# Another order-of-issue table for an attention and gated-MLP kernel on one Trainium2 core

## The chip, the core and the metric

The kernel runs on one core of a Trainium2 chip. The metric is the device time of one execution in microseconds (us), lower being better; the time stated is the median of several executions. The profile is one further execution, recorded by the hardware profiler: start and end of every instruction of the five engines (TensorE or PE, VectorE or DVE, ScalarE or ACT, GpSimd or POOL, SyncE or SP) and of the DMA packets.

## The reference

A residual block on x of 2048 tokens by 512 features, in float32. A layernorm feeds two branches, full softmax attention with 32 heads of 16 features, and a gated MLP of width 1792; the output is x + attention * silu(MLP).

```python
def reference(A_x, A_wqkv, A_wo, B_x, B_w1, B_w3, B_w2):
    xn = _layernorm(A_x)                       # 1 x 2048 x 512
    q, k, v = heads(xn @ A_wqkv)               # 32 heads of 16
    p = softmax(einsum("bhqd,bhkd->bhqk", q, k) * 16 ** -0.5)
    s = merge(einsum("bhqk,bhkd->bhqd", p, v)) @ A_wo
    h = silu(xn @ B_w1) * (xn @ B_w3)          # 2048 x 1792
    g = silu(h @ B_w2)
    return A_x + s * g
```

(The names heads and merge stand here for the reshapes and transposes of the original.)

## The kernel before

Operands of the matmuls are split into a high and a low part in a rounded format (float32r), and a product of two such pairs is three matmuls. Only the exponentials times the values are multiplied in plain float32.

There are three stages. The first normalizes and transposes x, makes queries, keys and values and spills them to DRAM. The main stage, which begins 160 us after the first instruction in the profile, works on attention and the MLP at once. The last multiplies by the output weights (`o` in the table), joins the branches and stores.

In the main stage attention goes through 32 phases, a phase being a pair of heads p and a half of the queries (1024). There are four kinds of work for TensorE, and each has a letter:

- `m` / `M` (`max_unit`, line 389): scores of 128 queries by 512 keys into one PSUM bank; VectorE reduces them to a row maximum (line 391). The maxima belong to the phase that comes next.
- `s` / `S` (`scores`, line 627): scores of 128 keys by 512 queries, with the maximum already subtracted by two extra rows of the operands; ScalarE takes the exponential from the bank (line 630) into one of 23 buffers `pt`.
- `v` (`values`, line 640): a value block. Four matmuls multiply four such buffers (two heads, two groups of queries) by 17 columns of values (16 and a column of ones), each in its own 32-column stripe of the array, into the bank `pv`. In plain float32 each is two records in the profile, so a block has eight. 16 blocks make a phase, 512 all of them.
- `f` / `F` (`Lanes.emit`, line 858): the MLP's matmuls, in units of 128 features.

The first, second and fourth kind use half of the array's rows each. A small letter is the lower half (rows 0 to 63, lane 0), a capital the upper half (rows 64 to 127, lane 1). A matmul of each half can run side by side; such a pair is called a slot below. An f product's contraction of 128 is cut into a lower and an upper half; the upper follows the lower into the same bank, and only then is the product done. Value blocks, transposes and the output's products use the whole array, so the halves stop for them. A stretch of whole-array matmuls between two stretches of halves is called a turn.

Seven PSUM banks go around (`take` gives the one that comes free first by the planner's account), and one, `pv`, holds the value sums. So an s or m waits until ScalarE or VectorE has read the bank's last content. A GpSimd pair of instructions splits each unit of MLP weights (lines 321 and 322).

The order in which the kernel issues all this is written out by hand: `ORDER_OF_ISSUE`, a string of letters. The loop at the end of the kernel's function goes through it. An entry that can't go yet (no exponential buffer, no bank, its inputs not due) is put on the list `late` and tried again before each later entry. `r` stands for a value block just ahead of which the finished row maxima of a phase are transposed (`second`, line 404), and `R` for that transposition alone. A small planner (`Model`) keeps due times of banks, lanes and engines while the program is built; they decide what is ready, and when small steps and DMAs are put into the other engines' queues. At run time nothing of it is left but the order of the instructions on each engine, and semaphores.

Of the kernel before, what the change touches and what calls it, by code (L numbers as in the profile page):

```python
# [50 lines left out]
    "MffSfMfSfMfSfSfMfSfMfMfSfMfsMsFFfFffFsMMfMfsFFfFfMsfFfFMsfFmFmFvmMmMFsFffFfFfMFsfFFfFffMSfMffFFmFmfS"  # L51
    "vFmfSFmFfmFfFSfFmFmfFfSfFFmFsFfFfMfMffMMsvSfMfsFfFmFsFMffMsFfFfMsFfFsFMfFsfFMfFfMmvSmmSmFFmvSmmSFmvS"
    "ffMMffSfSFffMSfFfmFsFmFmFFsfFfMfMFmvvSfmMMfFffFsFsFFfFfFsMfsFfFMsfFMfmFSffFMmvSfMfSffMFfSfMffSmFFfsF"
    "mFFsmFFfsFmFmFmFvvvrSfMfSffMfSfSfMsFfFmFsFFmFsFmFsFsFfMfsFfMfSfSFmvmSSmmSvSsmSfMmvfMmSsFmFfFFfSfMfsF"
    "mFFfsFmFfFsFsFMmvvmSMffSMfSffSfMfSfMffMsFFfsFmFFfsFFmFsMffFsFFfMfFmfSmSvSmsSMmvsMMmsFsFvSmsMsMvmSsFs"
    "FMfFffFMsFfmFSfMfFfsMfFFfSfMfSfmFvmSMmmFmFvvvsMfSfFSffMfFFsfMFsfFsMFfFsmFSffFmSFffSrvsMfMfSFffFsFmFf"
    "SFmsFfFfMsFFmFsFmFfSmvmSfSMsMfvmSMmMsvvfMfSSfMfSffMfSfFfMfFsFmFsFsFmFfFsFmFsFfMfFfSmMfSfsMffSsvmSSff"
    "MsMvsSmSmMvvSfMffSfMfSfSfMfMfFfFmFsFfFfFsMfFfSmSfFfFmFsFmFmFsFfFsFfFmSfFmFsFfFfMfMfMsMvsMfMMsvsMSmFm"
    "vSmmFFmmFmFmFvvvmSmFfFFmsFFfmFsFFfsFfMSfFfMfSfMfMfSfFffMsFFfSfMfSfFfMfsFsRvvSmMffSfSfMffSfSmFfFsFmFs"
    "FFfMfFsFfsMFffSMffSfFmSfFsFMfFfSfmFsFsFmFFfmFsFSffFmMvSmsSmMvsFmSmSmFvvmFSmsMsFvsMFmMssFvsMMmsSvsFmS"  # L60
    "FmmSvSmfFmSfSfFFfmSfFmFsFFffSmFsFfFMsfFSfMffFFsmMvsMMmmFmFvvvsMfSfFMfFffSmSfFmFsFfFMfSfMfFfsMfFFssFr"
    "vvSmfFSfFmfSFfmSfFsFMfsFFfmFSffFMsfFFsMffSFfMffMMfsFFfFfMsfFFmFsFfMfmFsFFfMfmFFfMsvvSmsSSmvmSsMvvMff"
    "SSffFMfFssFmFfFsFMfsFFfMfSfmFsFFffFfMSffMSffSfMfFsFfMsFfFmFsFsFmFfFsFmFmFfSmvmSmSSfvmSmMMsvSmSmvSmSf"
    "FfMffFSfmSFfMfsFfFmFsFFfMfsFmFFmFfMfmMvvvMsMsfFfFFsfFMsfFsFFfmFFssFFfMfSffSsFrvvSfMffSfMSffSfMfMfFfS"
    "fFsFmFfFsFmFsFmFsFfFsMfSfFmMvSmmSmFFsvSmmSMsvMsMfsFsFfFFfMsfFFsmFSffFMsFffMfFMfSfMsvmSMmfSvvMfSsfFmF"
    "FfFsmFFfsFMfSffSmFFffSMfFfSfMmvSmFmmFsFvSmmSMsvSmmFfSSffFfFmSfFsFMfFsfFMsfFFsMffSFfMmvSmFmMmvvSfMffM"
    "fSfSfSfMfFfFsFmFsFfFmSfFsMfFfFmFsFmFmMvvrsMFfsFMfFsFfMsFfsFMfSfFfmSfFmFsFmFfFMfMfmSvvSfMfMffSfSfMfSf"
    "FfMfFsMfFsFfMfFsFfMsFsFfFmFsFfMmFfMfSvSmsMMsvSmmSfMvsMMmSffSvvMffSfMfSfMfSfSfFfFmFsFmFsFfSfMfFsFmSFf"
    "FmSfFsFmFfFsMfMfFsMfFsFFsFfFfMfSfMssFvSmMmFsvSmFsmFmSvSmmMsSvSmFsFsmMvSmmFmFsFFmmFmFvvvMsfSMffSfFfFs"
    "MfFFsMffSFffMsFfSMffMFfSfFfSfsMFfFffSSfsSRvvvsMfMMfSffFFffMsFfFFsfMsFfFMfsFmFSfmFFfSffSfFmFmFsFFmFfs"  # L70
    "FmFFfSffMFfsMvvSmSsMmvSmMmfSvvMfmSFmFsfFfFsFmFFfsFsFmFsFFfmFsFFfMsFfsFMfFsFfmMfFSfSfFmvvSmmSfSFfFfFf"
    "mFfSfMfSFffMsFmFfFsFmFMfmFFfMsvvsMfSsFFmFffFMsFfSfmFFsFfsMFfmFfSFfFsmMvSmmSSfvMssSmMvMsSfMfSmvmSMmSs"
    "vvmSfSSfMfFffFSfMffSSfmFFfsFmFFfFsmFsFfMsFmFsRvvSmFfMfSffMFfMfSffFmFmFsFFfFsMfFffFsFFmMmvsMFmsSvMssS"
    "mMvvmFFssFsMFfFfMffSfFMsfFSfMfsFfFmSFffFfSmSvMmsFfFfFfSFmfSfFSmfFfSmFSffFmSfFmFSfmFfFmMvSmMssFvmSsMM"
    "svmSmFsFfSfFFmsFFfmFSfmFfSFmfFMsFfmMvvsMMssMvMsMsfSMfvvMfSffMMfMffSfMfSffFfFsFmFfFsFsFFmFsFffMsFFfMm"
    "RvSmSfSffMfFfFmSfFfSmFsFfFMsfFmFsFMffFsFSfMmvsMMmmFvvSfmFfSSfmFfFSfmFsFFfmSFfFsmFFsFfMmFffMSfvsMfSMs"
    "vvMfSsFfFmFsfFsFmFfFsFsFMffFmFSffFMfmMvvSfMffSfMSffSfMfSfFfFmFsFmFsFfFsFmFfFsMsFfMmFvsMfSfMmSvSmfSsF"
    "FmfFfFsMFffSmFSfFfMsfFmFsFmFfFMfMfMmvvfSMmMmvvsMFmFsFfFsFfmFsFfFsFMfSfMfSffFfMsFsFMfRvMsfMSffSfSfMSf"
    "vMsMfSfSsvmSSfmMvMsSfSfMsvmSfSFfFmFfFsmFFsmFFfsFFmsFFmFfSffMfMSfFffSMfSffFSfmFsFFfmSfFsFMfMffFmMvsMf"
    "MmMvvmMsMFsFsvsMSmSmvsMFsfFSmFffFmFSfmFfSFffMsFFmfFsMFfSffFFmSfFsMfMfFfsFMffFsFfFMfsSvMfSssMMfvsMmMS"  # L80
    "svSmFmmSvSmmFmMmFvvvmSfFsFmFFsfFSmFfsFFmFsfFSmfFmFmFsFFfsFFmFffMSfMfSffMSfRvsMfMfSMfSffMfSfMfSvSmfMs"
    "FsFFfFfMsFfsFmFFsfFmSfFMfmFsFFfsMvSmmSFfFfsFFfmFSfsFmFmFvvvvmSfFFfsSMffFFfFsmFFsfSfMFfFsFmFmfFmSvSmM"
    "mfMSfvSmSfMsvMsMfsFFfFsFfMsFfsFmFfSfFmSfFfSFmfFmFsSvmSSfMfsMvsMmMMmvvvfSMffSfMSffSFfmFsFFfmSfFsFfFMf"
    "SfsFsFmFFfsFrvMsfMfSfFfSFffMfSFmFsMfFfSfmFfFsFmFFfsFmFmMvsMFfsFFmFsFfsFMfSfSfmFFffSmFSffFmFFmMfvSmMs"
    "SfMfvsMMsSsvmFSmSmvvMffSfMfFsMFffSfMFfsFSfmFSfFfmFfFsFFmFffSMfsFfFFmfFSfmFsFfSmFFfmFSfFmfFSfmFmMvvsM"
    "sMsMvsMMfMsvSfMsFmFsFfFfmFFsFmfFSmFfSfMfFfsFMfMfMfFfMmvvvsMSffSfFfFmFsFfFsFmFFsFffSMfFfSfSmFfSfsFrvv"
    "SmfSfFFfSmfFSmFfSffFSmfFSffMsFFfMfsFmFFmFffMsFfFmFFsfFfSmFfSfFFmsFmFfMFsFfmMvmSfSSmvMsMsMsvsMfMMfSsv"
    "sMMsMsvvMffMSfMffSfFsFfFmFsFmFmFSffFmFsFFfmFMffSvsMSsSmvMfMsfFFssFFfmFFsFfsFmFSffSmFfFfSMffMfFSmvmSM"
    "fsMvSmsSFmmFvSmmSMmvvmSSfSfmFfFFfMsfFFsMfsFfFMsfFMffSsFfFMffMfSSffSfMrMsMsvSmmMsSvvSfMffSSffMfMfMfSf"
    "MfsFfFfFFsFmFsFmsFFfMfsFfMfFMsfFFmSfFffMsFmFFfSfmFfFSfmFfFmSvvSmsSmFFmvSmSmMmvvmFsFMfmFsFFfFsFmFfSff"  # L90
    "MFssFfFMfSffMfSfFfSmFfFsFMsFfFsMfFffMFffSfMSmvvsMmMsMvvSfMfSffMfMfSfMfFsFfFsMfFsFfFsMfFmFsFsFfFmFfSf"
    "MmFfSfSfFmFfSfFmFsFmFfSmFfMmvvMsSssFvrvSmfSSfmFfFfFmSFfFsmFFsFfmFsFsFsFmFfFFfmSFfmFsFFfmFSsfFmMvvSmS"
    "sMmvsMMsSfvmSMsSsvmFSfMfFfsMFfFsmFFfSfmFFfSffMfFsFmFfFMmfMvvMffMfSfSfSfFMffFsFFfMsFfFsmFfFFsmSfFFmmF"
    "vsMMmSfvsMsFFfMfFsFfmSFfSfmFFsfFmSFfmFSfSffFMfmFMmvvSsMsmMvvsMfMfSFffSfMSffMfSfMfFsFsFfMFfsFmFsFmFmF"
    "FmFmFsvvsMfFFmsFfFFmMfsFfFfSFfMsFfSfMfFfSfMfFsMRvvsMMffSSffFFfMsFfSfMfsFfFmFsFFmsFFfmFFmfSmSvSmmSSmv"
    "SmMfsSvMssMSmvsMsFFmFfFfSmSfFfMfSfFmSfFfFmSfmFFsmFfFMmvvMsfSMfsMvMsmSsSvMsFmsFsFfFfFmFSffSmFFsFfMfsF"
# [1257 lines left out]
```

## Time and profile before

| | |
|---|---|
| time before, median of 3 runs | 1739.95 us (1739.35 to 1740.43) |
| span of the profiled execution, first to last instruction | 1737.7 us |
| TensorE busy | 1730.3 us, 100% of the span |
| VectorE busy | 1432.1 us, 82% |
| ScalarE busy | 1254.2 us, 72% |
| GpSimd busy | 765.5 us, 44% |

The profiled execution's own time is not listed apart from its span; the median of the timed runs lies 2.25 us above that span. A line of the profile names the source line, the engine, the operation, the tiles as out<-in, the shapes and the count; PEld is the loading of weights into TensorE, which runs beside its matmuls. Ends of matmuls are modelled, so that a matmul of 512 columns is shown with some 0.39 us while the next one of the same half starts 0.23 us after it. Starts are to be trusted.

### The profile page before, as it was taken

The numbers are of one execution on the slowest core, as the hardware profiler recorded it, in microseconds if no ns is written. First come the engines' busy times: TensorE is split into PE (matmuls) and PEld (weight loads), VectorE is DVE, ScalarE is ACT, GpSimd is POOL, SyncE is SP. The second block draws the span as 40 slices with busy tenths as digits, with TensorE's granted clock in tenths as the row PEclk, the third lists the DMA queues.
The fourth block names the chain that finished last, engine by engine and source line by source line (L and its number), as shares of the span: only waits on it lengthen the run. The fifth ranks groups of instructions, "written<-read, shape, count | busy, mean of one in ns | idle before, by whom it ended". The sixth has DMA issues, their size and how long they took to land.

```text
span 1737.7 us, 35616 instructions
## 1 busy us (share of the span) xinstructions
PE 1730.3 (100%) x13236; PEld 1044.5 (60%) x13236; DVE 1432.1 (82%) x2349; ACT 1254.2 (72%) x2440; POOL 765.5 (44%) x793
## 2 busy tenths in 40 slices
PE   9999999999999999999999999999999999999999
PEld 7877656565665555555655655565655555566456
DVE  7567989888888889789888888888988988888535
ACT  4223787878878787778778877887788777777762
POOL 3103653365535560566265623644455515661201
PEclk9999999999999999999999999999999999999999
DMA  8657213122323121222423221132523222421542
GB/s 288 241 205 206 65 33 68 50 69 63 80 84 91 53 72 28 69 66 75 105 74 68 57 63 52 46 72 56 135 56 68 70 35 55 115 76 37 180 152 97
DMA packets 147373, 155.36 MB, mean 89 GB/s; under 512 B 42368, under 2 KB 101760, under 8 KB 144224
## 3 DMA queue, kind: packets, MB, share of 16 engines
q1 hardware_dynamic: 146336, 152.04, 31.7%
q8 instruction: 104, 1.70, 0.4%
q10 hardware_dynamic: 864, 1.05, 0.2%
q14 instruction: 69, 0.57, 0.1%
HBM read 107.97 MB, written 44.02 MB: 87 GB/s over the span
## 4 chain that ended last, share of the span: by engine, by line
PE 98%; DMA 1%; DVE 1%; SPq 0%; ACT 0%; issue 0%; POOL 0%; POOLq 0%; ACTq 0%
PE f L858 28%; PE pv L640 27%; PE e L627 17%; PE m L389 14%; PE m L507 3%; PE e L195 2%; PE e L199 2%; PE e L197 2%; PE o L195 1%; PE o L199 1%; PE o L197 1%; PE m L480 0%; PE m L404 0%; DMA wl<-g 0%; DMA ovl<-o 0%; PE o L1089 0%
## 5 line engine op out<-in xcount | busy, mean ns | idle before, releaser
L391 DVE TENSOR_REDUCE mp<-m 128x1 f32<-128x512 f32 x2048 | 1298.5, 684 | 164.2 <-PE m L389 89.8
L630 ACT ACTIVATE pt<-e 128x512 f32<-128x512 f32 x2048 | 1085.7, 606 | 268.4 <-PE e L627 121.2
L627 PE MATMUL e<-qs,ks 64*128 64x512 f32 x2048 | 716.0, 411 | 0.0
L389 PE MATMUL m<-ks,qs 62*128 62x512 f32 x2048 | 697.8, 413 | 0.0
L640 PE MATMUL pv<-pt,vt 128*17 128x512 f32 x4096 | 508.7, 596 | 0.0
L627 PEld LDWEIGHTS e<-qs,ks 64*128 64x128 f32 x2048 | 344.6, 185 | 228.7 <-ACT pt L630 85.0
L389 PEld LDWEIGHTS m<-ks,qs 62*128 62x128 f32 x2048 | 334.7, 184 | 141.0 <-ACT pt L630 42.8
L640 PEld LDWEIGHTS pv<-pt,vt 128*17 128x17 f32 x4096 | 84.0, 96 | 206.7 <-issue 199.9
L858 PE MATMUL f<-xth,wh 64*128 64x512 f32 x488 | 171.1, 392 | 0.0
L858 PE MATMUL f<-xth,wl 64*128 64x512 f32 x488 | 170.8, 396 | 0.0
L858 PE MATMUL f<-xtl,wh 64*128 64x512 f32 x488 | 169.7, 392 | 0.0
L743 POOL TENSOR_TENSOR h<-g,h 128x512 f32<-128x512 f32 x56 | 72.0, 1286 | 198.8 <-ACT h L739 198.8
L858 PE MATMUL f<-wh,hs 64*128 64x512 f32 x496 | 157.3, 394 | 0.0
L858 PE MATMUL f<-xth,xel 64*128 64x512 f32 x408 | 146.7, 394 | 0.0
L858 PE MATMUL f<-xth,xeh 64*128 64x512 f32 x408 | 143.1, 393 | 0.0
L858 PE MATMUL f<-xtl,xeh 64*128 64x512 f32 x408 | 142.5, 392 | 0.0
L858 PE MATMUL f<-xeh,hs 64*128 64x512 f32 x400 | 122.7, 393 | 0.0
L322 POOL TENSOR_TENSOR wl<-wr,wh 128x512 fp32r<-128x512 f32 x92 | 118.5, 1288 | 7.7
L322 POOL TENSOR_TENSOR xel<-wr,xeh 128x512 fp32r<-128x512 f32 x76 | 98.0, 1289 | 6.3
L727 POOL TENSOR_SCALAR th<-th 128x512 f32<-128x512 f32 x56 | 34.7, 620 | 143.2 <-ACT th L720 143.0
L321 POOL TENSOR_SCALAR wh<-wr 128x512 fp32r<-128x512 f32 x92 | 57.2, 621 | 86.5 <-PE f L858 85.5
L321 POOL TENSOR_SCALAR xeh<-wr 128x512 fp32r<-128x512 f32 x76 | 47.3, 622 | 101.0 <-PE f L858 48.2
(179 smaller groups left out, 2089.5 us busy)
## 6 DMA issues: line engine op xcount, KB each, us to landing
wr<-in_B_w_dram SPq DMA_DIRECT2D x168, 256.0 KB
qs<-qk SPq DMA_DIRECT2D x186, 64.0 KB
ks<-qk SPq DMA_DIRECT2D x90, 128.0 KB
qk<-sh SPq DMA_DIRECT2D x32, 256.0 KB
qk<-sl SPq DMA_DIRECT2D x32, 256.0 KB
v<-vrow SPq DMA_DIRECT2D x16, 272.0 KB
xin<-in_A_x_dram SPq DMA_DIRECT2D x16, 256.0 KB
g<-part SPq DMA_DIRECT2D x16, 256.0 KB
```

Of the source, the lines that this page charges most:

```text
L195: nc.tensor.matmul(ps, lhs[1], rhs[0], start=first, stop=False)
L197: nc.tensor.matmul(ps, lhs[0], rhs[1], start=False, stop=False)
L199: nc.tensor.matmul(ps, lhs[0], rhs[0], start=False, stop=last)
L321: nc.gpsimd.tensor_scalar(hi, t, 1.0, 1.0, op0=ALU.mult, op1=ALU.mult)
L322: nc.gpsimd.tensor_sub(lo, t, raw(hi))
L389: nc.tensor.matmul(ps, qs[p % 2][64 * h:64 * h + KM, q0:q0 + P], ks[p % 2][64 * h:64 * h + KM, c * 512:(c + 1) * 512], start=True, stop=True)
L391: nc.vector.reduce_max(mp[p, half][:, h, qt, c:c + 1], ps, axis=AX.X)
L627: nc.tensor.matmul(ps, ks[p % 2][64 * h:64 * h + KR, k * P:(k + 1) * P], qs[p % 2][64 * h:64 * h + KR, q0:q0 + 512], start=True, stop=True)
L630: nc.scalar.activation(pt, ps, AF.Exp, scale=DH ** -0.5)
L640: nc.tensor.matmul(pv[32 * j:32 * j + VW, :], vt[2 * p // GH][:, key, 2 * p % GH + j % 2, :], pt, start=key < 2 if last else k == 0, stop= ...
L743: nc.gpsimd.tensor_mul(h2, g, h2)
L858: nc.tensor.matmul(ps, left[r], right[r], start=starts and lane == 0, stop=ends and lane == 1)
```

## The change

The string `ORDER_OF_ISSUE` is replaced by another. Nothing else is touched. Both strings hold the same amount of each kind of work: 2016 f and 2016 F, 1024 s and 1024 S, 992 m and 992 M, 22 o, and 512 value blocks (v and r together). Three things differ.

The value blocks stand in 279 runs instead of 356. Counted in the strings by the letters v and r alone, the old one has 351 (227 of one block, 91 of two, 29 of three, 4 of four) and the new one 279 (98 of one, 134 of two, 42 of three, 5 of four).

The transpositions of row maxima all stand with a value block: 31 r and no R, in place of 18 r and 13 R.

The letters of the two halves are mixed more freely. In the old string no more than two letters of one lane follow each other; in the new one there are rows of three (545 of them), four (184), five (62) and up to nine.

The head and the end of both strings:

```diff
 ORDER_OF_ISSUE = (
-    "MffSfMfSfMfSfSfMfSfMfMfSfMfsMsFFfFffFsMMfMfsFFfFfMsfFfFMsfFmFmFvmMmMFsFffFfFfMFsfFFfFffMSfMffFFmFmfS"
-    "vFmfSFmFfmFfFSfFmFmfFfSfFFmFsFfFfMfMffMMsvSfMfsFfFmFsFMffMsFfFfMsFfFsFMfFsfFMfFfMmvSmmSmFFmvSmmSFmvS"
...
-    "vorSsSsovSsSsSsSovsSSssSosSSsSsvvSsSssSvvoSsSsSsvovSssSsosSsSovSsSsovsSovsSSsoSvvvoooooSssSSsoSsoosS"
-    "sSosSSsvvvv"
+    "fffMffFfFSfffMSfSfFfMSMMSMsffsMMFffFsMffSFFmfFFsFsFmFFfmMfMfFFffMMFvvMssSmFffmfMFsfSfFFmfSMfFffmffSf"
+    "FSfMfFFMfFFffFFfMSsmsFfMsFmfFfSMFFFfsFfmMsfFmMvvmMMsMsvvMsMSFfffSFfmSfFmFfSfMfSfSFfmffFSmFFFfsFmFffs"
...
+    "SsMMsoSMMMssSvSMsMsSmoMssSsSvvmSMSMssvmSmSSMsvSSSmMmsvMsMsSsMvSmMSsMsvsmSSSSosvvSsssSMvrSssSSssssoSS"
+    "SosSSssSvvvSsSsSSsvvvSsssSSoosSosSSsvvosSSSssvvvsSSssSosSsSSsvvsSSsSsoooSoSsssSooovvooossSSSoovvvv"
 )
```

More of the change, by code (lines that the diff above doesn't have):

```diff
@@ L56 @@
[L56 to L60, printed above, removed]
@@ new lines @@
+    "FFMSmfFSFFFFsmsfFSmfFfMFsFfFmFFmFmMFmvvSmSfSmMfvMSmmSsvMsmsSfFffffMSFmFsFmFFsfFMFfsfMsffffMFFMMMsvvs"
+    "sMmFFsFfFfFSmfFsMFfFsfFSmfFmSFffFSfMfMfMmFvvmSmFFsSMvvmMmsFSSvrSfMSMFffSfffFfMfSsmsfmFsmFFsfsffFfMSF"
+    "ffMfFSMfSfFmfFFsFFmsFFFmsfMfSfmfFFFmFmmSvvSsMmFMmFvFvMFSsfsMMfvmMSFsSmvSmFmsssmFmFfSffFmSfFFFmfSfmSm"
+    "vsMsMsMvsfMfMMFSsvSmMssMvMsMfSSfFFffSfffffMFfSMMMffMMfsMvFvMsFsmsFsmsmFFfffSFmSFfFmfsFfMsffFFSMfmffF"
+    "SfSffFMffSfMSFmfFSfFMfFSmfmMFFvrFMsmsfsFfMsFfffMFSMFFfsmffFfSFSmFFFsfmsFFFFfFmsmsfFFFmffMfMffMMmMFvv"
@@ new lines @@
+    "vSmSSmmvsFfffMSffffMfFFSMfSMSmfsmSFmFfFFfFsFFmmsffmFSFfFsFmSFfmFsfFmFFfMmFMMMMFmvvmFfsMfvvsfMffMfSMf"
+    "SffSfMSFFfsFmfsmFfFMFssFfFmFsfmfFSFFsmFsFfmFSfmFsFmFFfmMvrMmmMsSvvmSMmMmvvfSSFFmfmFfFFsmSfFFFFmfsmSf"
+    "MffFSFfffMmFMFfMmvvmSMFfSfFfFFsmFsmsfFFmSFFffFmssFMFFmvsMSFmSmvMffSMSfSfffMfSffFMSffMfSfsmsFmffSFmfS"
+    "FFFmSFFsFfssfSsvvvSFmFSfFFsFFmfmsfFsFmfSfFsfMFmffFSffFMSMfmSvssfMMmMMMvvMsssvsfMmFSSFffFfMsfFFsMfffS"
+    "FSFFFmfmsFFfmSFmfmMvrFFMMsFmFsSvMffFSfFfMfSffMSsFmsfmsmfSFmFffSFFmffFMFmmMvvSmFsFmsFFFmmFsFfFfsMffSM"
@@ new lines @@
+    "fffFfSMSfffFFMmMFfFMmvvvMFsfMFsfssMffFsMFfsFfMsFfMsfFFmSfMFfFfmfMSsvmSmMsSvSFmmsSffFfFMffSFmFSffSFmm"
+    "FFfFsMFffsFFmmMvvsMMsMsvMfsMfSmSvSmmSmMvrMsfSmFfFsffFfMSFfMsFfMsFfMFffSfFsMsFfFfFmFffMffSSfMFsFFFfmF"
+    "fSFFmfsFfSFmfFmFFfmmmSvvvSSmSmmvsMffSMfffFSMFsFfMsfFfSMFfFsfMsfFFsmFffsFFffMFMFSfFFFfmsfFsSFmfmfFfSF"
+    "MfFsfFmFFMsfmSFvvvsMMSSfFfffmFFsfMsFFfsFmsffFFfMSmFSfFfMfSfsFsFSFvvSSSssFmvvSsSSmsvvMffSfffMSSffSFFS"
+    "fSvvSMsfmfSFFfmFfsMmFsmfsFfFFFsmfFFsmsffFFSfMsFMFfSfffMffSFFFffFFMMfMfmMvvrfSffMSfMfFfSsmfsMFsfFFmSf"
```

145 lines of the change are left out of this document (67 added, 78 removed).

## The prediction

> **What bounds the kernel now.** I read the page first, then the busy time of the main stage, then the chain of waits in one stretch of it, then single instructions in order of time.
>
> ```profile
> span 1737.7 us, 35616 instructions
> PE 1730.3 (100%) x13236; PEld 1044.5 (60%) x13236; DVE 1432.1 (82%) x2349; ACT 1254.2 (72%) x2440; POOL 765.5 (44%) x793
> PEclk9999999999999999999999999999999999999999
> L391 DVE TENSOR_REDUCE mp<-m 128x1 f32<-128x512 f32 x2048 | 1298.5, 684 | 164.2 <-PE m L389 89.8
> L630 ACT ACTIVATE pt<-e 128x512 f32<-128x512 f32 x2048 | 1085.7, 606 | 268.4 <-PE e L627 121.2
> L640 PE MATMUL pv<-pt,vt 128*17 128x512 f32 x4096 | 508.7, 596 | 0.0
> ...
> 160.00:1620.00 1460.00, 1460.00 (x11800) 856.41 (x11799) 1272.79 (x2071) 1145.58 (x2222) 722.84 (x737) 1.00 0.27 69
> ```
>
> The last line is the main stage (160 to 1620 us), the columns PE, PEld, DVE, ACT, POOL, granted clock, DMA share, GB/s: TensorE has no idle time that the profile can see, at full clock; VectorE is busy for 87% of it, ScalarE for 78%. So the order of the matmuls sets the time, and what must be priced is how densely they follow each other. "PE busy" does not tell that, since ends are modelled. Starts do; the chain of waits shows them:
>
> ```profile
> 49 pieces in order of time: start us, us, what
> 700.57 3.56 PE pv L640 x32
> 704.13 0.42 PE m L389
> ...
> 708.02 0.24 PE f L858 x2
> 708.27 0.22 PE e L627
> 708.49 0.02 PE m L389
> 708.51 0.98 PE pv L640 x8
> 709.49 0.43 PE e L627
> ```
>
> A value block is eight records (4096 for 512 blocks). One block alone holds the chain for 0.98 us, four in a row for 3.56, so a further block costs (3.56 - 0.98) / 3 = 0.86 us, and each run of blocks has 0.98 - 0.86 = 0.12 us on top. The first pair of half-array matmuls behind a run takes 0.42 to 0.43, a later pair 0.23 or 0.24 (0.24 for the two f at 708.02, one of each half). So entering the halves again costs 0.43 - 0.23 = 0.20 more. One turn (halves, values, halves) costs 0.12 + 0.20 = **0.32 us**, whatever the length of the run.
>
> As a test of these prices on the main stage: between 160 and 1620 us the program has 3979 slots (pairs of halves; of a stretch with unequal halves the longer one), 480 blocks (the x3840 below), 329 turns and 30 small transposes of row maxima.
>
> ```profile
> L640 PE MATMUL pv<-pt,vt 128*17 128x512 f32 x3840 | 476.9, 596 | 0.0
> ...
> L404 PE MATMUL m<-ident,nm x32: 271/277/278, 151.0 to 1646.7; 128*16 128x128 f32 x32
> ```
>
> 3979 x 0.23 + 480 x 0.86 + 329 x 0.32 + 30 x 0.28 = 915.2 + 412.8 + 105.3 + 8.4 = 1441.7 us. The stage took 1460, so all waits of TensorE for operands and banks come to about **18 us**, 0.055 us per turn.
>
> **The change, part by part.** Work is the same: the counts of s, m, f and value blocks do not change. Three things do.
>
> Turns. The table goes from 356 runs (351, when the letters v and r alone are counted) to 279. What counts is the built program, since an entry that cannot go when its turn comes is caught up later: from the first scores on, it has 356 whole-array stretches before and 283 after. 73 fewer x 0.32 = **-23.4 us**. These lie on TensorE's own order, with nothing beside them that could have hidden them. A part of it is that all 31 second steps of the row maxima now stand beside a value run (r) and none by itself (R, 13 before); it is in the count.
>
> Lanes. In the old program no more than two halves of the same half of the array follow each other, and the two halves of nearly every stretch are equally many. In the new one up to eight follow each other, and more stretches are unequal. If each half of the array takes its next matmul as soon as it is free, a stretch costs as many slots as its longer half has: 4085 slots in the whole program before, 4101 after. 16 x 0.23 = **+3.7 us**. But that holds only if a matmul can overtake those of the other half that stand ahead of it in the queue and still wait. The old order hardly asks for it; single instructions show that it happens:
>
> ```profile
> start us, us, engine line op out<-in xcount [idle before <-releaser]
> 1602.28 0.18 PEld L389 LDWEIGHTS m<-ks,qs 62*128 62x128 f32 x1
> 1602.38 0.19 PEld L858 LDWEIGHTS f<-wh,hs 64*128 64x128 f32 x1
> 1602.46 0.39 PE L389 MATMUL m<-ks,qs 62*128 62x512 f32 x1
> 1602.62 0.39 PE L858 MATMUL f<-wh,hs 64*128 64x512 f32 x1
> ...
> 700.94 0.12 PEld L640 LDWEIGHTS pv<-pt,vt 128*17 128x17 f32 x4 [0.31 <-issue]
> 701.37 0.12 PEld L640 LDWEIGHTS pv<-pt,vt 128*17 128x17 f32 x4 [0.31 <-issue]
> ```
>
> In the program the F with operands wh,hs stands directly ahead of this m. The m loaded its weights 0.10 us and started 0.16 us before it. So the halves are not held to the program's order, for one place at least. How far it reaches, the value runs tell, where four column stripes play the part of the two halves. Each of a block's four matmuls is two records (first and second pass), in the program stripe by stripe. Yet at 700.94 the first passes of the second block load their weights on all four stripes within 0.12 us, and the second passes 0.43 us later. So the load of stripe 3 went past six matmuls that had not started (both passes of stripes 0, 1 and 2), two on each stripe. The new program, with free halves, never asks a half to go past more than six. I count the slots also for less, a half being held back until all but k of those ahead of it have started:
>
> | k | 0 (strict order) | 1 | 2 | 3 | 4 | 5 and more |
> |---|---|---|---|---|---|---|
> | slots after (before: 4085 for each k) | 5038 | 4402 | 4199 | 4132 | 4108 | 4101 |
>
> The bounds of this term are so 16 and 953 slots, 3.7 and 219.2 us. I take 3.7, since six were passed in the row at 700.94; what those rows don't show is more than two waiting matmuls of one stripe being passed, and that is the first rival. [...]
>
> Where the work stands. The new table finishes the f earlier: behind the last f stand 48 value blocks, 171 s and 58 m, before 31, 114 and 13. Up to the first product of 12 whole-array matmuls that is 88 slots, 29 blocks and 24 turns: 20.2 + 24.9 + 7.7 = 52.8 us of TensorE (two transposes and two small sum steps not counted), with 99 exponentials of 1085.7 / 2048 = 0.53 us on ScalarE, 52.5 us. That is nearly level, where before ScalarE had slack, so part of TensorE's time can turn into waiting for pt and banks: 0 to +8 us, I take **+3**. VectorE has 58 x 0.63 = 37 us there, which is covered. SP's and POOL's instructions keep their kinds and counts; only what the f need comes a little sooner against the end:
>
> ```profile
> L322 POOL TENSOR_TENSOR wl<-wr,wh 128x512 fp32r<-128x512 f32 x92 | 118.5, 1288 | 7.7
> L321 POOL TENSOR_SCALAR wh<-wr 128x512 fp32r<-128x512 f32 x92 | 57.2, 621 | 86.5 <-PE f L858 85.5
> ```
>
> One unit of weights takes POOL 0.62 + 1.29 = 1.91 us, and the 24 halves that use a gate or up unit take at least 12 x 0.23 = 2.8 us, even with nothing between them. So POOL, 44% busy, keeps up at no cost; if it did not, the first late unit would hold the f for up to its 1.91 us.
>
> The waits. Score and maximum matmuls wait for one of seven banks, which ScalarE and VectorE empty:
>
> ```profile
> PEld e L627 <- ACT pt L630: 85.0, 112, 0.9
> PEld e L627 <- DVE mp L391: 61.9, 79, 0.9
> ```
>
> These are idle times of the weight loader, mostly beside a running matmul; only the 18 us above reached the chain. Runs of two blocks become the rule, so ScalarE and VectorE run dry more often within a run and have the same work in less time: VectorE's 1272.8 us of 1460 become 1272.8 of about 1443, 88%. On the other hand each stretch of halves begins with empty banks, and there are fewer such beginnings. Bounds: -4 us (0.055 for each of 73 turns that go) to +18 (they double). The s and m among the first eight halves behind a run are 5.1 on average in both programs, so I take 0.
>
> **The sum.** -23.4 + 3.7 + 3 + 0 = -16.7 us. On the profiled execution, 1737.7 - 16.7 = 1721.0 us of span; the median of the runs lies 2.25 us above that span, so 1739.95 - 16.7 = 1723.2, given as **1723**.
>
> **Rivals.**
>
> *A shallow lane (slower).* The rows above show two waiting matmuls of one stripe being passed, not three. If a half of the array holds only two and then stops the queue for both, k is 2: 4199 - 4085 = 114 slots, 26.2 us, in place of 3.7: -23.4 + 26.2 + 3 = +5.8, 1746 us. The point from which it decides is 23.4 / 0.23 = 102 extra slots, between k = 2 and k = 3; with k = 3 the sum is -9.6, 1730 us, still in the forecast's range. For it: no stretch of the old program has three halves of one lane in a row. Against it: at 700.94 six were outstanding in all. With k = 1 it would be 317 x 0.23 = 72.9: +52.5, 1792 us; the same rows speak against that.
>
> *Strict order (much slower).* If matmuls start in the order of the program, k is 0: -23.4 + 219.2 = +195.8 (the tail's 3 us are lost in it), 1936 us. [...] The rows at 1602.46 and 1602.62 disagree: the later matmul started 0.16 us earlier.
>
> *The waits double.* With VectorE at 88% and longer runs, the 18 us become 36: -16.7 + 18 = +1.3, 1741 us. For it: both idle rows above end on the bank's reader. Against it: equal numbers of s and m behind each run.
>
> That the change does not do what it says is settled by the built program, 283 stretches for 356.
>
> **How the numbers follow.** Forecast, with the lanes free or k at least 3: 0.58, its own range 1714 to 1735 (below: -23.4 + 3.7 + 0 - 4 = -23.7, 1716, and 2 for the rounding in 0.32; above: k = 3 with 10.8 for the slots and the tail's +8, -4.6). Waits double or nearly: 0.19, of which 0.04 come out faster, 0.05 the same, 0.10 slower. Shallow lane with k = 2: 0.14, of which 0.03 the same, 0.11 slower. k = 1: 0.05. Strict order: 0.04. About 0.2% (3.5 us) is what a measurement of this kernel can tell from no change. Faster: 0.58 + 0.04 = 0.62; same: 0.08; slower: 0.10 + 0.11 + 0.05 + 0.04 = 0.30. The range goes from 1714 to 1756 (the shallow lane's 1746 with half of the 18 us of waits on top); it leaves out k = 1, strict order and some 0.07 at both ends.
>
> **What the profile after would show.** Value runs that still cost 0.98 for one block and 0.86 for each further one, and first pairs behind them of 0.43: the price of a turn. Pairs of 0.23 inside stretches where three and more halves of one lane stand in a row, with starts that differ from the program's order by several places: free lanes. A pair every 0.35 us or so in such stretches, and stretches longer than their longer half: a shallow lane, and the forecast is wrong by its sign. Idle rows of the weight loader behind ACT pt and DVE mp well over 85.0 and 61.9 us with the slots unchanged: the waits. DVE over 82% of the span, at the same 1298.5 us for the maxima: the same work in less time.

## The result, and the profile after

The changed kernel is slower: 1832.12 us (1829.27 to 1832.44, 4 runs) against 1740.19 us for the kernel before beside it, ratio 1.052, 95% interval 1.051 to 1.054. The forecast was 1723, with 1756 as the upper end. The profiled execution has a span of 1830.1 us, 92.4 more than before. (The changed kernel's string has one row less, so its line numbers are one lower: m is L388, the maximum L390, s L626, the exponential L629, v L639, f L857.)

From the page: the span, the engines' busy time, the chain that ended last by engine (for comparison first the chain of the kernel before, which was not shown yet, then that of the changed one), and the groups of the two readers and of m.

```profile
PE 98%; DMA 1%; DVE 1%; SPq 0%; ACT 0%; issue 0%; POOL 0%; POOLq 0%; ACTq 0%
```

```profile
span 1830.1 us, 35699 instructions
PE 1799.2 (98%) x13236; PEld 1107.3 (61%) x13236; DVE 1425.3 (78%) x2349; ACT 1258.8 (69%) x2440; POOL 763.6 (42%) x793
PE 90%; DVE 3%; issue 3%; ACT 1%; DMA 1%; POOL 1%; SPq 1%; POOLq 0%; ACTq 0%; DVEq 0%
L390 DVE TENSOR_REDUCE mp<-m 128x1 f32<-128x512 f32 x2048 | 1292.6, 684 | 289.1 <-PE m L388 138.9
L629 ACT ACTIVATE pt<-e 128x512 f32<-128x512 f32 x2048 | 1092.3, 605 | 374.9 <-PE e L626 177.1
L388 PE MATMUL m<-ks,qs 62*128 62x512 f32 x2048 | 729.6, 427 | 10.7 <-DVE mp L390 8.3
```

The readers do the same work in the same time per instruction (684 and 605 ns), but stand idle for longer ahead of it: 289.1 us for 164.2 and 374.9 for 268.4. The chain that was TensorE's for 98% is so for 90%. So TensorE waits for the readers, and the readers wait for TensorE. "PE busy" hardly shows it (98%), as ends are modelled.

The price of a turn is where it was. The chain of waits between 1235 and 1243 us, its short pieces left out:

```profile
1235.94 2.70 PE pv L639 x24
1238.64 0.43 PE m L388
1239.08 0.23 PE m L388
1239.31 0.24 PE e L626 x2
1239.56 0.98 PE pv L639 x8
1240.54 0.66 PE f L857 x2
1241.97 0.69 DVE mp L390
1242.71 0.50 PE e L626
```

0.98 for one block, (2.70 - 0.98) / 2 = 0.86 for each further one, 0.43 for a first pair, 0.23 for a later one. But then VectorE takes over the chain for 0.69 us. The same place instruction by instruction (behind [ ] idle time and what ended it) shows why:

```profile
1240.47 0.50 PE L857 MATMUL f<-wh,hs 64*128 64x512 f32 x1
1240.80 0.40 PE L857 MATMUL f<-wl,hs 64*128 64x512 f32 x1
...
1240.81 0.50 PE L388 MATMUL m<-ks,qs 62*128 62x512 f32 x1
...
1241.04 0.39 PE L857 MATMUL f<-wh,hs 64*128 64x512 f32 x1
...
1241.27 0.39 PE L857 MATMUL f<-xeh,hs 64*128 64x512 f32 x1
...
1241.50 0.39 PE L857 MATMUL f<-xel,hs 64*128 64x512 f32 x1
...
1241.96 1.89 DVE L390 TENSOR_REDUCE mp<-m 128x1 f32<-128x512 f32 x3 [0.96 <-PE m L388]
1242.00 1.08 ACT L629 ACTIVATE pt<-e 128x512 f32<-128x512 f32 x2 [1.28 <-PE m L388]
...
1242.71 0.18 PEld L626 LDWEIGHTS e<-qs,ks 64*128 64x128 f32 x1 [0.91 <-DVE mp L390]
1242.71 0.50 PE L626 MATMUL e<-qs,ks 64*128 64x512 f32 x1 [0.46 <-DVE mp L390]
```

The program's letters here are fffffMSMfMS. The M starts at 1240.81, past three f that still wait for the lower half (those at 1241.04, 1241.27 and 1241.50), 0.34 us after the first f, though nothing ran on its own half. So M overtook three here; what e4 shows of the limit is below. But VectorE, idle for 0.96 us, begins M's maximum only at 1241.96: 1.15 us after M's own start and 0.46 us after the start of the last f ahead of M in the program. ScalarE stands idle for 1.28 us in the same way. The banks come free that much later, and at 1242.71 TensorE has stood 0.46 us for one. The semaphore by which TensorE tells its readers rises in the same trace at 1241.91, 1241.94, 1241.97 and 1242.01, for the fifth f and the first three capitals, whose matmuls started between 1240.81 and 1241.50.

So this is the theory, drawn from these times (theory 1 in the expectations): **a half starts out of order** (M at 1240.81, past three f), **but its completion counts in the program's order** (behind M's start the first increment is at 1241.91, 0.41 us after the start of the last f ahead), and its reader starts by the latter (1241.96). Over all 4096 readings, the time between a matmul's start and the latest start ahead of it in the program (the readers' lead in the table below) sums up to some 8 us before and 304 us after; over 150 ns are 1 before and 788 after. (Matmuls of the same name are laid to the two halves so that no half starts two within 0.2 us.) Of those after, whose reader was idle: from the own start to the reader 887 ns (ScalarE) and 843 ns (VectorE), medians; from the latest start ahead 495 and 463, about as in the kernel before with nothing overtaken (534). The view of waits points the same way: readers of s and m banks released by an f, which writes a bank that they don't read. Before, after, and the first experiment below:

```profile
DVE mp L391 <- PE f L858: 16.6, 25, 1.7
ACT pt L630 <- PE f L858: 21.0, 31, 1.8
```

```profile
DVE mp L390 <- PE f L857: 56.6, 102, 4.8
ACT pt L629 <- PE f L857: 45.8, 95, 2.2
```

```profile
DVE mp L390 <- PE f L857: 5.7, 13, 1.8
ACT pt L629 <- PE f L857: 10.9, 25, 2.1
```

### The profile page after: what moved, and what is told of

It reads as the page before. It is cut to its first block, busy times and chain, and to the rows that moved or that the text cites. A ratio compares the mean times of both kernels' runs of the same rounds, so it can differ in the third digit from the quotient of the medians.

```text
span 1830.1 us, 35699 instructions
## 1 busy us (share of the span) xinstructions
PE 1799.2 (98%) x13236; PEld 1107.3 (61%) x13236; DVE 1425.3 (78%) x2349; ACT 1258.8 (69%) x2440; POOL 763.6 (42%) x793
## 4 chain that ended last, share of the span: by engine, by line
PE 90%; DVE 3%; issue 3%; ACT 1%; DMA 1%; POOL 1%; SPq 1%; POOLq 0%; ACTq 0%; DVEq 0%
PE f L857 25%; PE pv L639 24%; PE e L626 15%; PE m L388 15%; PE m L506 2%; DVE mp L390 2%; PE e L194 2%; PE e L198 2%; PE e L196 2%; ACT pt L629 1%; PE o L194 1%; PE o L198 1%; PE o L196 1%; PE m L403 0%; PE m L479 0%
## 5 line engine op out<-in xcount | busy, mean ns | idle before, releaser
L390 DVE TENSOR_REDUCE mp<-m 128x1 f32<-128x512 f32 x2048 | 1292.6, 684 | 289.1 <-PE m L388 138.9
L629 ACT ACTIVATE pt<-e 128x512 f32<-128x512 f32 x2048 | 1092.3, 605 | 374.9 <-PE e L626 177.1
L388 PE MATMUL m<-ks,qs 62*128 62x512 f32 x2048 | 729.6, 427 | 10.7 <-DVE mp L390 8.3
L626 PE MATMUL e<-qs,ks 64*128 64x512 f32 x2048 | 734.3, 421 | 4.1 <-ACT pt L629 1.6
L639 PE MATMUL pv<-pt,vt 128*17 128x512 f32 x4096 | 501.0, 598 | 0.0
L388 PEld LDWEIGHTS m<-ks,qs 62*128 62x128 f32 x2048 | 336.0, 184 | 192.3 <-DVE mp L390 72.6
L626 PEld LDWEIGHTS e<-qs,ks 64*128 64x128 f32 x2048 | 342.9, 185 | 168.7 <-DVE mp L390 59.2
L639 PEld LDWEIGHTS pv<-pt,vt 128*17 128x17 f32 x4096 | 90.0, 96 | 217.1 <-issue 206.0
L857 PE MATMUL f<-xth,wl 64*128 64x512 f32 x488 | 177.8, 399 | 0.0
L857 PE MATMUL f<-xtl,wh 64*128 64x512 f32 x488 | 177.4, 396 | 0.0
L857 PE MATMUL f<-xth,wh 64*128 64x512 f32 x488 | 175.4, 396 | 0.0
L857 PE MATMUL f<-wh,hs 64*128 64x512 f32 x496 | 155.0, 397 | 0.1
L857 PE MATMUL f<-xth,xeh 64*128 64x512 f32 x408 | 151.7, 397 | 0.0
L857 PE MATMUL f<-xth,xel 64*128 64x512 f32 x408 | 150.4, 399 | 0.0
L857 PE MATMUL f<-xtl,xeh 64*128 64x512 f32 x408 | 147.4, 395 | 0.0
L857 PE MATMUL f<-xeh,hs 64*128 64x512 f32 x400 | 125.9, 397 | 0.0
L857 PEld LDWEIGHTS f<-xth,wl 64*128 64x128 f32 x488 | 87.3, 185 | 7.7 <-issue 1.3
```

The source lines that it names most:

```text
L388: nc.tensor.matmul(ps, qs[p % 2][64 * h:64 * h + KM, q0:q0 + P], ks[p % 2][64 * h:64 * h + KM, c * 512:(c + 1) * 512], start=True, stop=True)
L390: nc.vector.reduce_max(mp[p, half][:, h, qt, c:c + 1], ps, axis=AX.X)
L626: nc.tensor.matmul(ps, ks[p % 2][64 * h:64 * h + KR, k * P:(k + 1) * P], qs[p % 2][64 * h:64 * h + KR, q0:q0 + 512], start=True, stop=True)
L629: nc.scalar.activation(pt, ps, AF.Exp, scale=DH ** -0.5)
L639: nc.tensor.matmul(pv[32 * j:32 * j + VW, :], vt[2 * p // GH][:, key, 2 * p % GH + j % 2, :], pt, start=key < 2 if last else k == 0, stop= ...
L857: nc.tensor.matmul(ps, left[r], right[r], start=starts and lane == 0, stop=ends and lane == 1)
```

## The experiments

The rivals of theory 1: halves can pass only few waiting matmuls, and the lost slots cost the time (theory 2); longer value runs leave the readers dry and then queued, whatever the order of the halves (theory 3); passing costs TensorE itself time (theory 4). Each run's profile was summed up in the same terms, against the profile of before (e8 and e9 against e7): turns at 0.32, slots (the longer half of each stretch) at 0.23, the time of the stretches of halves over 0.195 + 0.2307 per slot (19.4 us before), and the time of value runs with a transposition over 0.125 + 0.8585 per block (6.8 before).

| run | turns | slots | waits in halves | at transpositions | sum | measured span | readers' lead, us |
|---|---|---|---|---|---|---|---|
| the change | -23.4 | +3.7 | +98.3 | +13.9 | +92.5 | +92.4 | 304 |
| e1 | -23.4 | +4.2 | +27.2 | +15.9 | +23.9 | +22.3 | 14 |
| e2 | 0 | +0.5 | +84.5 | 0 | +85.0 | +84.6 | 228 |
| e3 | -23.4 | +4.2 | +149.8 | +15.9 | +146.5 | +148.6 | 293 |
| e5 | -23.4 | +4.2 | +27.6 | +8.8 | +17.2 | +18.4 | 14 |
| e6 | -17.6 | +1.4 | +58.4 | 0 | +42.2 | +42.4 | 8 |
| e10 | -24.0 | +5.3 | +35.3 | +4.7 | +21.3 | +18.9 | 63 |
| e11 | -0.3 | +0.2 | +6.8 | +1.8 | +8.5 | +6.4 | 61 |
| e8 to e7 | -23.4 | +3.7 | +47.1 | +6.1 | +33.5 | +34.4 | 320 |
| e9 to e7 | -17.6 | +1.4 | +27.1 | 0 | +10.9 | +11.3 | 17 |

The last column is the sum of the lead just told (8 before, 15 in e7). The columns leave at most 2.4 us open. Slots that the change loses because a half passed no more than three (e4) stand among the waits: 31 x 0.23 = 7.1 of the 98.3.

**e1: the new table, the halves side by side.** Same turns, blocks and transpositions; within each stretch the letters are merged pair by pair.

```diff
-    "fffMffFfFSfffMSfSfFfMSMMSMsffsMMFffFsMffSFF..."
+    "fMfSfMfSfSfMfSfMfMfSfMfMsMfFfFsFfFfFsMfSfFm..."
```

> The new table's work in the order in which its program issued it, 283 turns, but within each stretch of halves the two lanes are merged pair by pair (one lower, one upper), each lane keeping its own order: 4103 slots. Theory 1 (completions count in the order of the program, so the reader of a half that overtook starts only when all matmuls ahead of it have ended; banks come free late): the loss goes, and the turns' gain stands: 1740 - 73 x 0.32 + 18 x 0.23 = 1721 us, 1714 to 1732. Theory 2 (a half can pass only few waiting matmuls of the other, slots are lost): the same 1721, since nothing has to be passed. Theory 3 (longer value runs make ScalarE and VectorE run dry and then queue, whatever the lanes' order): still about 1830, at least 1790.

Measured: 1761.49 us (1759.04 to 1761.81), ratio 1.012 (1.0105 to 1.0135). So 71 of the 92 us were the mixing of the halves, as theories 1 and 2 have it; the waits in the halves fell from 98.3 to 27.2. But 1721 was not reached; for the 40 us between, see e5 and e6. (In e1, e5 and e10 the order changes what is computed, in a part that is not known; instructions and their counts are the same, and they stand here for their times alone. e2, e3 and e6 compute what the kernel before computes.)

**e2: the old table, the halves mixed at random.** Turns as before, 356.

```diff
-    "MffSfMfSfMfSfSfMfSfMfMfSfMfsMsFFfFffFsMMfMf..."
+    "fMSffMSMffSfSffMfSMffMSffMfsMFsffFFfFMMsMFf..."
```

> The old table's work in its issued order, 356 turns as before, but within each stretch the two lanes are merged at random, with rows of one lane about as long as in the new table (three 536 times, four 233, up to nine). If all halves start as soon as their lane is free, the readers' matmuls stand behind later-starting ones by 260 us in sum, against 375 in the new table and 15 in the old. Theory 1: about 100 x 260 / 375 = 70 us slower than before, 1780 to 1830 us. Theory 2 with three passed: 4097 slots for 4085, +3 us, 1743; with two passed +21, 1761; with one +78. Theory 3: as before, 1740 to 1745.

Measured: 1824.73 us, ratio 1.0487 (1.0469 to 1.0504), within theory 1's 1780 to 1830. With the old table's turns, mixing alone brings the waits. The slots explain 0.5 us of it, and the value runs didn't change: neither theory 2 nor theory 3 gives any of the 85 us.

**e3: e1 with the lower half two slots ahead.** The same pairs, still the same slots for a half that may pass two.

```diff
-    "fMfSfMfSfSfMfSfMfMfSfMfMsMfFfFsFfFfFsMfSfFm..."
+    "fffMfSfMfSfSfMfSfMfMfSsMfMfMsFfFfFsFfFfMmSf..."
```

> As the paired kernel, but the lower lane runs two slots ahead in the program: L0 L1 L2 U0 L3 U1 and so on. No half must pass more than two waiting matmuls (4103 slots for any depth of two or more), but nearly every s and m of the upper lane stands behind two lower ones that start later. Theory 1: each such reader starts 0.46 us late, 740 us in sum, so slower than the paired kernel by 60 us or more, 1780 to 1900. Theory 2 with a depth of two or more: as the paired kernel, 1714 to 1732. Theory 3: as the paired kernel, whatever that is.

Measured: 1888.03 us, ratio 1.085 (1.0834 to 1.0867), 127 us over e1. With equal slots, that excludes theory 2.

**e4: bursts at the kernel's start.** Equal matmuls on both halves with nothing else to do: n of the upper half, then n of the lower half; and one of the lower half that ScalarE copies from, alone, behind and ahead of others.

```diff
+        for n in (1, 2, 3, 4, 5, 6, 8):
+            ...
+            for h, ps in ((1, upper), (0, lower)):
+                for _ in range(n):
+                    one(h, ps)
+        for n, first in ((0, 1), (3, 0), (3, 1), (6, 0), (6, 1)):
+            ...
+            nc.scalar.copy(mark, lower[:, 0:8])
```

> The old kernel with bursts of halves put ahead of its first matmuls, without waits: n upper halves and then n lower ones (n = 1, 2, 3, 4, 5, 6, 8), and one lower half behind or ahead of 3 or 6 upper ones, with ScalarE reading the lower one's bank. Its total time says nothing; the trace is read. Theory 2 with a depth of three: the first lower half of n = 4 starts with the first upper one, of n = 8 when the fifth upper one starts; with a depth of one it starts with the third from the end's predecessor, one slot before the last; free lanes: at once for any n; strict order: with the last upper one. Theory 1: behind 3 upper halves the lower one starts at once, but ScalarE's copy starts about 0.43 us after the start of the last upper one, 0.9 us after the lower one's own start; behind 6, 0.43 us after the sixth. Ahead of them: 0.43 us after its own start. If completions are told singly, 0.43 us after its own start in every case.

The bursts show starts and readers without the kernel's other work. For n = 8 (m is the upper half's bank, e the lower's), and then the copies: behind none, behind three, behind six.

```profile
17.24 1.42 PE L519 MATMUL m<-ks 64*128 64x512 f32 x5
18.28 0.49 PE L519 MATMUL e<-ks 64*128 64x512 f32 x1
...
20.89 0.49 PE L519 MATMUL e<-ks 64*128 64x512 f32 x1
...
21.42 0.17 ACT L537 COPY mark<-e 128x8 f32<-128x8 f32 x1 [19.40 <-PE e L519]
...
21.90 0.50 PE L519 MATMUL m<-ks 64*128 64x512 f32 x1
...
21.91 0.50 PE L519 MATMUL e<-ks 64*128 64x512 f32 x1
...
22.98 0.17 ACT L537 COPY mark<-e 128x8 f32<-128x8 f32 x1 [1.39 <-PE e L519]
...
24.86 0.96 PE L519 MATMUL m<-ks 64*128 64x512 f32 x3
...
25.43 0.50 PE L519 MATMUL e<-ks 64*128 64x512 f32 x1
...
26.61 0.17 ACT L537 COPY mark<-e 128x8 f32<-128x8 f32 x1 [2.47 <-PE e L519]
```

For n = 8 the free lower half starts at 18.28, 1.04 us late, with the fifth of the eight: three are left waiting ahead of it. For n = 4, where three are left waiting, both halves started together (10.49 and 10.50). So three waiting matmuls were passed in these bursts, not more (k = 3 of the prediction's table, 4132 slots). The changed kernel agrees: the starts in its whole trace can be laid to the two halves with three passed at most, and not with two. And the copy: 0.53 us after the start of a lone matmul (20.89 to 21.42), 1.07 when it has passed three (21.91 to 22.98), 1.18 behind six, where it had itself started 0.57 late (24.86 to 25.43). With the three or six put behind it in the program, it was 0.59 and 0.58. So in these bursts the reader waited for the matmuls ahead of its own in the program (1.07 and 1.18 us for 0.53), and those behind it added 0.06 us at most. A rival would be that the reader waits for a count to which the matmuls passed must add as well. Here they add nothing to it: in the trace's record of semaphores the lower matmul's own increment stands 0.50 us after its start when it is alone, 0.99 when it has passed three, and there 0.42 after the start of the last upper one.

**e5: e1 with the early transpositions later.** Where an r stood under 5 us behind its phase's last maximum, a later block takes it.

```diff
-    "...mSfSvrmSfSfM...SfSfMmvmMmMm..."
+    "...mSfSvvmSfSfM...SfSfMmrmMmMm..."
```

> The table of e1_paired (the new table's turns, 283, with the two halves side by side, 4103 slots) with one thing changed: where the transposition of a phase's row maxima stands less than 5 us behind the phase's last maximum, it is moved to a later value run. It tests what the 40 us are by which e1_paired stood above 1721. If the transpositions waited for VectorE and GpSimd and held TensorE (idle rows of 22 and 32 us of the weight loader in e1_paired), the time falls from 1761 by 10 to 20, to 1741 to 1751, and the rows before the transposition fall to the 4 us that they have before. If the 40 us are banks that come free late because longer value runs leave the readers dry (theory 3, now for what is left), the time stays at 1757 to 1765.

Measured: 1758.47 us, ratio 1.0105 (1.0091 to 1.0119); a few us and not 10 to 20. The view of waits, TensorE's own idle time before the transposition (L403), e1 first:

```profile
PE m L403 <- ACT nm L399: 10.1, 10, 2.2
```

```profile
PE m L403 <- ACT nm L399: 4.1, 5, 2.2
```

The transpositions do wait, and 7 of the 16 us there went with the move; the rest of it and the 27 us in the halves stayed. That bears out neither of the two expectations in full: the time stayed at 1757 to 1765, and the waits were only in part those at the transpositions.

**e6: the old table with fewer turns.** 60 neighbouring runs joined, the halves left as they were.

```diff
-    "...mFFmvSmmSFmvSffMM..."
+    "...mFFmSmmSFmvvSffMM..."
```

> The old table with only its turns lessened: 60 neighbouring value runs less than 2 us apart are joined (a block put off or brought forward past the halves between them), 301 turns in the built program for 356, 4091 slots for 4085, the halves side by side as before. By the price of a turn alone: 55 x 0.32 = 17.6 off, 6 x 0.23 = 1.4 on, 1724 (1720 to 1729). Theory 1 (completions in the order of the program, so that only the mixing of the halves costs) expects just that. Theory 3 (longer value runs leave ScalarE and VectorE dry, and they queue behind them, whatever the order of the halves) expects that 0.3 us or more per turn comes back as waits: 1738 or more. From e1_paired, where 73 turns went and 27 us of waits came in the halves, a case between them would be 1738 - 1 to 1744.

Measured: 1781.88 us, ratio 1.0239 (1.0225 to 1.0253): 42 us slower, where the price of a turn alone gave 16 less. The readers lead by 8 us only, as before, so theory 1 has no part in it. This is theory 3 in one form. The old table has 105 short stretches of s and m alone, of 2.9 slots on average, between whole-array stretches; six halves fit into the seven banks. Joined, they are twelve:

```profile
548.55 0.50 PE L388 MATMUL m<-ks,qs 62*128 62x512 f32 x1 [0.25 <-ACT pt L629]
...
551.66 0.50 PE L626 MATMUL e<-qs,ks 64*128 64x512 f32 x1 [0.15 <-ACT pt L629]
```

These rows are from the stretch MssSmMMsSfMfSmmSMmSs, which begins at 547.33 and has 18 s and m among its 20 halves: TensorE stands for banks, and the stretch took 2.25 us more than its ten slots. Over the whole trace the halves start 57 us later than their own half of the array allows (a mean of the two halves), and 47 of these end with a release by ScalarE or VectorE. So a single block between two such stretches was not just a turn of 0.32 us; it was 0.98 us in which the readers emptied the banks, at no cost to TensorE.

**e7, e8, e9: shorter reads of the banks.** Before, the change, and e6, with half the columns in the maximum and the exponential.

```diff
-        nc.vector.reduce_max(mp[p, half][:, h, qt, c:c + 1], ps, axis=AX.X)
+        nc.vector.reduce_max(mp[p, half][:, h, qt, c:c + 1], ps[:, 0:256], axis=AX.X)
-        nc.scalar.activation(pt, ps, AF.Exp, scale=DH ** -0.5)
+        nc.scalar.activation(pt[:, 0:256], ps[:, 0:256], AF.Exp, scale=0.01)
```

> The kernel before with shorter reads of the banks: the maximum and the exponential take 256 of the 512 columns (the value block reads the 256 columns twice), so ScalarE and VectorE hold a bank for less. It leaves half of that work out. It is there as the base of e8. Before has some 18 us of waits in its main stage: all theories expect 1715 to 1738.

> The changed kernel with the same shorter reads (half of the columns in maximum and exponential). If its 92 us are waits for banks whose readers started late (theory 1), a reader that holds the bank 0.2 to 0.3 us less makes most of them go: the difference to e7 falls from +92 to between -10 and +40. If passing costs TensorE itself time (theory 4: each matmul started out of the program's order makes the array or its queue lose a little, no bank being waited for), the difference stays between +80 and +100.

> e6 (the old table with 60 neighbouring value runs joined, 301 turns) with the shorter reads of e7 (half of the columns in maximum and exponential, that half of the work left out). In e6 the joined runs leave stretches such as mmSSmm, twelve scores and maxima in six slots with seven banks to go around, and the halves waited 57 us more than before. If these are waits for banks that the readers hold, they go with the shorter reads, and the price of a turn remains: 55 x 0.32 = 17.6 less and 6 x 0.23 = 1.4 more than e7's 1729, 1713 (1709 to 1722). If the price of a turn is not real, or the joined runs cost TensorE itself something, e9 stays at 1729 or goes over it, up to 1729 + 42 = 1771.

Measured: 1729.09, 1763.85 and 1740.13 us. In the groups of e8 a reading takes 421 and 386 ns instead of 684 and 605:

```profile
L390 DVE TENSOR_REDUCE mp<-m 128x1 f32<-128x256 f32 x2048 | 795.4, 421 | 681.9 <-PE m L388 317.3
L629 ACT ACTIVATE pt<-e 128x256 f32<-128x256 f32 x2048 | 710.4, 386 | 650.9 <-PE e L626 318.2
```

The change's loss fell from 92 to 35, with the halves overtaking as before (lead 320). TensorE's part in it is the same, so theory 4, which wanted 80 to 100, falls as the main cause: of the 98 us of waits in the halves at least 51 are banks. For the other 47 this run says nothing. The changed kernel's own trace says more. Its halves start 101 us later than their own half allows (mean of the two): 45 of these end with a release by ScalarE or VectorE, 14 stand behind such a wait, 16 are the slower starts next to a late one, and in 7 more than three were waiting ahead. The remaining 19 are not told apart, so a small cost of passing itself is not excluded.

e9 missed: it stayed 11 us over e7 where 7 to 20 less was expected, in the range named for a price of the turn that is not real or joined runs that cost TensorE itself something. Of e6's 58 us of waits 31 went. The trace of e9 still has 24 us of late starts, and 19 of them end with a release by ScalarE or VectorE, so the rest is banks too in the main. A shorter reading takes 421 and 386 ns in e8 for 684 and 605; that it leaves the time until it begins as it is (median 534 ns from a matmul's start to an idle reader in the kernel before) is the author's estimate.

**e10 and e11: both tables after a search** of single moves and exchanges, by the planner's account with theory 1's rule, three waiting halves, and a wait at the transposition. Of the first row of each:

```diff
-    "fMfSfMfSfSfMfSfMfMfSfMfMsMfFfFsFfFfFsMfSfFm..."
+    "SfMffMfSSffMMfSffSfMfMfsMffsffMsFfFMFFFfmSF..."
-    "MffSfMfSfMfSfSfMfSfMfMfSfMfsMsFFfFffFsMMfMf..."
+    "MffSfMSfMffSfSFfMfSffFMfSfMfsMMfFsffFfMsFMf..."
```

> The table of e5 after a search of single moves (a block to a neighbouring run, letters exchanged within some places) by the kernel's own planner, in which a reader's start is counted from the latest start of all halves ahead of it in the program, no more than three waiting halves are passed, and the transposition waits for its row maxima. 281 turns, 4108 slots. By that account the main stage falls by 14 us against e5 and ends 6 below the old table's; e5 itself was measured 10 above what the account says of it. Theory 1 with the seven banks: 1734 to 1748. If the count of turns were what the time depends on, 1720. If something else than banks and transpositions holds the new table back: 1755 or more.

> The old table after the same search: 355 turns, 4086 slots, single letters exchanged. By the account the main stage falls by 7 us, of which 3 to 6 are waits of transpositions that the account sees and the profile of before may not have. Expected 1733 to 1739. If the account has it wrong where lanes are mixed a little (planned lead of readers 67 us for 15), 1740 to 1760.

Measured: 1758.58 us, ratio 1.0105 (1.0089 to 1.012), and 1745.85 us, ratio 1.0033 (1.0021 to 1.0046). Both missed. e10 has 4 us less at the transpositions than e5 and 8 more in the halves, e11 7 us more in the halves; in both the lead is a little over 60 us. e11 lies where its expectation had put a cost of a little mixing for which the account finds room. e10 lies where its expectation had put something else than banks and transpositions, and that stays open; one such wait is told under e12. No table tried here beats the old one.

**e12: a tile of its own for the spread sums.** One wait of the changed kernel is not of this kind. Its largest, 7.2 of the 8.3 us in the group row above, is at its end:

```profile
1713.70 1.26 POOL L660 TENSOR_TENSOR ot<-ot,rb 128x512 f32<-128x512 f32 x1 [11.30 <-DMA rb<-rd]
1714.99 0.43 DVE L1091 COPY rb<-rec 128x512 f32<-128x512 f32 x1 [8.61 <-POOL ot L660]
...
1716.07 0.79 PE L388 MATMUL m<-ks,qs 62*128 62x512 f32 x1 [7.22 <-DVE mp L390]
```

VectorE's queue stands at a copy that overwrites rb, GpSimd reads rb late, since its DMA was issued late (at 1710.25 in SP's queue, behind loads and stores), and the maxima wait behind VectorE's copy. The same chain stands in e1, where VectorE's copy waits 5.9 us and TensorE 4.4 behind it. Each kernel here with the new table's end has a stretch of halves that waits 5 us or more there (6.2 us in e1, 5.2 in e5 and e10, 7.3 in e3, 7.9 in e8); before and e6 have none over 1 us.

```diff
-        nc.vector.tensor_copy(rb.rearrange("p (a b) -> p a b", b=32),
+        nc.vector.tensor_copy(spare().rearrange("p (a b) -> p a b", b=32),
```

> The changed kernel with one difference at its end: the reciprocal sums of the last three phases are spread by VectorE into a tile of their own in place of rb. In the changed kernel's trace VectorE stands 8.6 us before that copy (it overwrites rb, which GpSimd reads once the DMA rb<-rd has landed, 11.3 us of idle time there), and TensorE stands 7.2 us behind VectorE's next maximum. If that chain is what holds it, the time falls by 6 to 9 us, from 1832 to 1823 to 1826, and the idle time of 7.2 us before a maximum matmul is gone. If the wait was of something else (a bank or operands that come at the same time), the time stays at 1829 to 1833.

Measured: 1833.82 us, ratio 1.0537 (1.0519 to 1.0554), no gain. The wait is gone from that copy and back at another instruction of VectorE; TensorE's idle time grew from 7.2 to 9.8:

```profile
1721.52 0.71 DVE L1066 TENSOR_SCALAR oh<-ot 128x512 fp32r<-128x512 f32 x1 [9.77 <-DMA o<-oh]
```

```profile
PE e L626 <- DVE mp L390: 11.2, 6, 9.8
```

It now waits for stores from the buffer oh, which SP issues behind the same DMAs. What both waits have in common is SP's queue; a kernel with that queue in another order was not tried.

## Why the prediction was wrong

**The turns, -23.4:** right as a price. 73 fewer at 0.32, and the rows of the chain have the same 0.98, 0.86, 0.43 and 0.23. That nothing stood beside them was wrong: the readers worked there (e6).

**The lanes, +3.7:** the size was off, the kind right. Halves overtook, but past three waiting matmuls (e4, n = 4 and 8), not six or more; with k = 3 the term is 47 slots, 10.8 us (7.1 more, which the table counts among the waits), a case that the text gave within the forecast. The row at 700.94, from which six were taken, is of weight loads on the value stripes; it did not carry over to the matmuls of the halves, and why is not settled. The shallow lane (k = 2) and strict order didn't come about.

**The waits, 0 (-4 to +18):** the step that failed. They were +98.3, some 10 of them in the tail (below). The reason given for 0, equal numbers of s and m among the first halves behind a run, counts what stands there and not when its banks come free. Two things were missed.

The larger, 71 us: the text asked whether a half may *start* ahead of its turn, and stopped there. What an s or m is for is a bank that another engine reads and frees, and that hangs on when the reader starts (in the changed kernel 1.15 us behind M's own start at 1240.81). The row at 1602.46 showed starts out of order and nothing of readers. The rival of strict order was weighed by the starts at 1602.46 and 1602.62 alone. On starts the runs go on to speak against it (three waiting matmuls passed in e4); the readers kept to the program's order (1.07 us to a passing matmul's copy, 0.53 to a lone one's), and that decided.

The smaller, 27 us in e1: fewer and longer value runs are not only fewer turns. The 18 us of waits of before were spread over the turns as a loss of each; e6 shows that in the old table the single blocks kept the waits low, by giving the readers time between stretches that the seven banks could hold. So the bound of +18 (they double) had no ground in the rows: it scaled a remainder that a different arrangement had made small. Of the 27 us in e1, 7.5 stand behind the last f and are the wait told under e12 in the main; 18 stand ahead of 1590 us, spread over the main stage. That these 18 are what e6 shows is argued and not shown by a run of their own.

**The transpositions:** "it is in the count" was wrong. By the price of a turn (0.32 us) an r beside a value run saves a part of one, an estimate; but the new table puts several close behind the phase's last maximum, whose way goes over VectorE, ScalarE and back: 13.9 us in the change, and e5 took 7 back from e1's 15.9 by their place alone.

**The tail, +3 (0 to +8):** about +10 in its halves, and for another reason than ScalarE being level: the one wait of 7.2 us behind VectorE and SP's queue. That SP's instructions "keep their kinds and counts" was true and did not help; their order against VectorE's had changed.

**What was to show it:** the sign named for the waits, idle rows of the weight loader well over 85.0 and 61.9, was a poor one. The rows of m before, and then all four after:

```profile
PEld m L389 <- ACT pt L630: 42.8, 61, 0.9
PEld m L389 <- DVE mp L391: 32.9, 59, 0.9
```

```profile
PEld m L388 <- DVE mp L390: 72.6, 123, 7.5
PEld m L388 <- ACT pt L629: 64.5, 146, 0.9
PEld e L626 <- DVE mp L390: 59.2, 112, 0.9
PEld e L626 <- ACT pt L629: 53.2, 94, 1.2
```

249.5 us in all against 85.0 + 61.9 + 42.8 + 32.9 = 222.6 before: 27 more, for 98 lost. Loads that wait beside a running matmul and loads that hold TensorE are added up in one number. And DVE's share fell to 78% where over 82% was named for a faster kernel.

## What to carry to other kernels

Where a trace shows matmuls on parts of the array overtaking each other, look at their readers as well as at their starts: here a half passed up to three waiting matmuls, and the readers of those that overtook started 0.46 to 0.50 us (medians) after the latest start ahead in the program. So starts were to be planned by each part of the array and readers by the program, and what another engine waits for should have stood no later in the program than it was to run; mixing the halves cost 71 us. And before merging small pieces of work to save a switch, ask what ran beside the switch: here a turn of 0.32 us bought the readers a block's 0.98 us, and taking out 55 turns cost 42 us.

## What the runs showed of the hardware that was not expected

In e4 a free half started past three waiting matmuls of the other half without delay (10.50 against 10.49 at n = 4), and at n = 8 it started 1.04 us late (18.28 against 17.24), when three were left waiting. In the changed kernel, readers behind a matmul that passed others started 0.50 us (ScalarE) and 0.46 us (VectorE), as medians, after the latest start ahead of it in the program; in e4 it was 0.50 us, where the matmuls passed write another bank and nobody waits for them.
